# Attention with routed feed-forward on one core: the main loop's matmuls in couples of 64 rows

## The chip, the cores and the metric

The kernel runs on one core of a Trainium2 chip. The metric is the device time of one execution in microseconds (us). Three runs of the kernel before gave 2052.83, 2055.91 and 2057.64 us; the median is 2055.91 us. One more execution was recorded by the hardware profiler; all rows shown here come from that one. TensorE is called PE in the rows, its loading of the stationary operand PEld, VectorE DVE, ScalarE ACT, GpSimd POOL, and the queue that issues transfers SP.

## What is computed

Eight batches of 3136 tokens; `u` and `v` have 256 features a token, `z` has 64. All is float32.

```python
scores = scale * np.matmul(z, z.transpose(0, 2, 1))      # scale = 1 / 3136
attn = np.maximum(scores, 0.0) ** 2
out = np.matmul(attn, v)
x = u * out
...
top_idx = np.argpartition(-(x[b] @ w_gate), 128)[:128]   # for each batch b
xe = x[b, top_idx]
ye = np.maximum(xe @ w1, 0.0) @ w2                       # w1: 256 x 1024, w2: 1024 x 256
x[b, top_idx] += sigmoid(scores of top_idx)[:, None] * ye
```

## The kernel before

**Numbers in two halves.** Every float32 operand of a matmul is split into a high part (rounded to the matmul's type `F32R`) and a low part (the rest). The tensors are `ZH`, `ZL` for `z`, `V[...][w]` with w = 0 (high) and 1 (low) for `v`, and `hi`, `lo` for the squared scores. A product of two such numbers keeps the terms high x high, high x low and low x high.

**Chunks and slots.** The queries of a batch are cut into six chunks of 512 (`CH`) and a last one of 64 (`WHOLE`). The keys are cut into 24 tiles of 128 and one of 64. A slot is a pair of key tiles for one chunk of queries: first its scores, then its products. Since the scores are symmetric, pairs left of the diagonal aren't computed again: the squared scores are turned by DVE, kept in DRAM (`squares`) and fetched (`qk`).

**Scores.** `z` has only 64 features, and a matmul can contract over 128 rows. `ZH` and `ZL` therefore hold their 64 rows twice, in partitions 0 to 63 and 64 to 127, and the moving tile `Z` holds the queries' high part in its upper 64 rows and the low part below, brought there by two transfers a chunk (`bring_z`). One matmul with `ZH` gives high x high plus high x low; a second with `ZL` gives low x high plus low x low. A pair of key tiles takes four matmuls of 512 columns into the two banks of a score tile `sc`; two such tiles exist (`sc_ring`).

**Squares.** ACT reads the score tile (`rise`, `a<-sc`: relu), squares it into `hi`, and then DVE, which multiplies the score tile by `a`, or ACT makes the full square in `a`; only then the score tile is free. POOL or DVE subtracts to make `lo`.

**Products.** The output is kept transposed: 128 features (`h` = 0 or 1) by 512 queries in one PSUM bank `acc`. For each key tile and h there are three matmuls of 128 rows and 512 columns: `V` high and low with `hi`, `V` high with `lo`. Three banks rotate. At a chunk's end DVE multiplies the bank by `ut`, the transposed `u` (`finish`, `evict`).

**The order of the work** is fixed when the program is built: a class `Clock` estimates when each engine would be done, jobs wait in lists for ACT, DVE, POOL and SP, and `choices` takes the next matmul group that would be ready: scores first, then steps of the routing and feed-forward (the `chains`), then products of the current and the next slot. On the chip every engine simply runs its list in order and waits on semaphores. All instructions show one line, L230, that of the recording helper.

Of the kernel before, what the change touches and what calls it, by code (L numbers as in the profile page):

```python
# [18 lines left out]
P = 128  # L19
CH = 512  # L20
GT = 4
# [14 lines left out]
WARM = 6.6  # L36
REST_AT = (2, 5, 7, 9, 12)
# [47 lines left out]
class Clock:  # L85
# [3 lines left out]
    def __init__(self):  # L89
        self.at = {"pe": 0.9, "act": 1.15, "dve": 0.85, "pool": 0.5, "sp": 0.75}  # L90
        self.queue = self.mark = 0.0
        self.writes, self.reads, self.before, self.rings = {}, {}, {}, {}
        self.port = {"dve": (0.0, 0.0), "pool": (0.0, 0.0)}
        self.newest = {}

# [83 lines left out]
    def note(self, by, op, outs, ins):  # L179
# [8 lines left out]
        elif by == "pe":  # L188
# [6 lines left out]
            self.at["pe"] = begin + took + (0.1 if n < 200 else 0.002)  # L195
# [94 lines left out]

class Job:
# [15 lines left out]
def attention_then_routed_ffn(ctx: ExitStack, tc: tile.TileContext, zt, ut, v, wg, w1, w2, cst, cst16, keys, outs, at, cap):  # L307
# [29 lines left out]
    ps_s = Pool(clock, "ps_s", ctx.enter_context(tc.tile_pool(name="ps_s", bufs=2, space=bass.MemoryType.PSUM)), 2)  # L337
# [3 lines left out]
    sc_ring = Ring(ps_s, [P, 2, CH], "sc", 2)  # L341
# [7 lines left out]
    moving_ring = Ring(const, [P, CH], "Z", 2)  # L349
# [4 lines left out]
    banks = [[ps_a, f"acc{i}", None] for i in range(3)]  # L354

    def bank_when():

        free = [clock.idle(x[2][1:]) if x[2] else 0.0 for x in banks if x[2] is None or x[2][0] == "-"]
        return min(free) if free else None

    def take_bank(name):

        x = min((x for x in banks if x[2] is None or x[2][0] == "-"), key=lambda x: clock.idle(x[2][1:]) if x[2] else 0.0)
        got = x[0].tile([P, CH], F32, name=name, tag=x[1])
        x[2] = "+" + got.name
        return got

    def drop_bank(tile_):
        for x in banks:
            if x[2] == "+" + tile_.name:  # L370
                x[2] = "-" + tile_.name
                return
        raise AssertionError(tile_.name)
# [232 lines left out]
    Z = {}  # L606
# [27 lines left out]
    def prep_z(b, i, rank, of=None):  # L634
# [13 lines left out]
        pieces = [slice(0, GT // 2), slice(GT // 2, GT)] if b == i == 0 else [None]  # L648

        def high(e):  # L650
            round_on(e, to[0], src)
            for x in pieces:
                job("pool" if x else "pool|dve", rank, lambda e, x=x: low(e, x), [src, to[0]], took=takes(n))

        def low(e, x):
            at_ = (lambda y: y[:, :, x]) if x else lambda y: y
            rest_on(e, at_(to[1]), at_(src), at_(to[0]))
            if x is pieces[-1]:
                zdone[b, i] = True
                ring.drop(st)  # L660
            for t in range(*x.indices(GT)) if x else ():
                zdone["tile", t] = True
# [16 lines left out]
        free = lambda: b == 0 or (issued > last_key[b - 1, i] and (b - 1, i) in Z)  # L679
        job("act", rank, high, lambda: clock.after(src) + (SLACK if b else 0.05), ok=free)  # L680

    def bring_z(b, c):

        c0, w = CHUNKS[c]
        t = moving_ring.take("Z", F32R)
        Z[b, c] = t[:, :w]
        for rows, z in ((slice(0, 64), ZH), (slice(64, P), ZL)):
            nc.sync.dma_start(t[rows, :w].bitcast(F32), z[rows, c0 : c0 + w].bitcast(F32))

    def first_z():  # L690

        t = moving_ring.take("Z", F32R)
        Z[0, 0] = t
        st = staged["z", 0, 0].rearrange("p (f t a) -> p f t a", t=GT, a=Q)
        to = by_rows(t, 0, CH)
        nc.vector.tensor_copy(to[:64], st[:64])
        nc.vector.tensor_tensor(to[64:], st[64:], by_rows(ZH, 0, CH)[64:].bitcast(F32), op=ALU.subtract)
# [52 lines left out]
    for b in range(B):  # L750
        for c in range(WHOLE):
# [13 lines left out]
            if c < WHOLE - 1:  # L765
                seq.append(half)
# [132 lines left out]

    def own_rest(k, ps):  # L900
# [3 lines left out]
        def rise(e):  # L904
            a_.append(a_ring.take("a"))
            nc.scalar.activation(a_[0][:REST, 0, :REST], ps[:REST, 0, :REST], AF.Relu, scale=SCALE * SCALE)
            job("act", k, high, [a_[0][:REST, 0, :REST]], (), lambda: "own_rest" in consts)

        def high(e):
# [4 lines left out]
            job("dve", k, square, [a, ps[:REST, 0, :REST], st[:REST, :REST]])  # L914

        def square(e):
            a = a_[0][:REST, 0, :REST]
            st = parts[k][0]
            nc.vector.tensor_tensor(a, ps[:REST, 0, :REST], a, op=ALU.mult)
            sc_ring.drop(ps)  # L920
# [6 lines left out]
    def can_score(k):  # L927
        b, c, js, _ = slots[k]
        if k == 0 and not all(("tile", j) in zdone for j in js):
            return False  # L930
        return sc_ring.free() and (b, c) in Z and (k == 0 or all((b, j // GT) in zdone for j in js))

    def score_when(k):
        b, c, js, _ = slots[k]
        t = max([sc_ring.when(), clock.after(Z[b, c])])
        return max([t] + [clock.after(z[:, j * P : (j + 1) * P]) for j in js for z in (ZH, ZL)]) + 0.05

    def half_scores(k):
# [4 lines left out]
        nc.tensor.matmul(ps[:, 0], ZH[:, NJ * P : (NJ + 1) * P], Z[b, c], start=True, stop=True)  # L943
        if k == last_moving[b, c]:
            moving_ring.drop(Z[b, c])
        st = {}

        def shift(e):
# [3 lines left out]
            job("dve", k, total, [st["a"], ps[:REST, 0]])  # L952

        def total(e):
            nc.vector.tensor_tensor(st["s"], ps[:REST, 0], st["a"], op=ALU.add)
            sc_ring.drop(ps)
# [48 lines left out]
        job("act", k, shift, [ps[:, 0]], [a_ring])  # L1005

    def scores(k):
# [4 lines left out]
        mov, w = Z[b, c], CHUNKS[c][1]  # L1012
        if is_second(k):
            mov, w = mov[:, w // 2 :], w // 2
# [8 lines left out]
        if k == last_moving[b, c]:  # L1023
# [1702 lines left out]
```

## Time and profile before

| | |
|---|---|
| median of three runs | 2055.91 us |
| the profiled execution | 2054.14 us |
| its span, first to last instruction | 2052.4 us |
| PE busy (records overlap, so it is no measure of load) | 2041.8 us |
| PEld busy | 1676.7 us |
| DVE, ACT, POOL busy | 1459.0, 1406.9, 1065.8 us |
| mean granted TensorE clock | 1.000 |

A matmul's record reaches from its start to the modelled end of its results; the next one starts before that end. What a matmul costs in a stream is the distance from its start to the next start, called the pitch here.

### The profile page before, as it was taken

The page shows a single profiled execution, that of the slowest core. Times are in us where ns is not written, and L with a number is a line of the kernel's source. Part 1 is how long each engine was busy: PE and PEld are TensorE (multiplying, and loading weights), DVE is VectorE, ACT ScalarE, POOL GpSimd, SP SyncE. Part 2 cuts the span into 40 slices and gives each one's busy share as a digit, 9 for nine tenths or more (in the row PEclk, how much of TensorE's full clock was granted, in tenths as well). Part 3 has the DMA queues.
Part 4 walks back from the last instruction along what each step waited for, and adds up shares of the span by engine and source line. Part 5 has one row for each costly group of instructions (what it writes and reads, how often), then busy time and mean ns, then how long its engine had stood idle before and what let it go on. Part 6 is the DMA issues. An engine that isn't in the chain of part 4 may idle for free. (4 is left out here: it accounts for less than half of the span.)

```text
span 2052.4 us, 29009 instructions
## 1 busy us (share of the span) xinstructions
PE 2041.8 (99%) x9248; PEld 1676.7 (82%) x9248; DVE 1459.0 (71%) x2424; ACT 1406.9 (69%) x1654; POOL 1065.8 (52%) x704
## 2 busy tenths in 40 slices
PE   9999999999999999999999999999999999999998
PEld 7888888888888888888888888888888888888777
DVE  8875577656887568666688666886667666698876
ACT  7875687656876568766777656776678765876652
POOL 6564743447644474245754457433573245754553
PEclk9999999999999999999999999999999999999999
DMA  7898767777678877777777797688777769766774
GB/s 222 245 272 224 191 201 213 209 183 194 195 216 229 209 185 206 221 206 186 197 212 202 207 228 187 210 231 237 190 196 221 203 173 212 214 198 177 185 169 126
DMA packets 430345, 420.00 MB, mean 205 GB/s; under 512 B 131694, under 2 KB 332016, under 8 KB 430192
## 3 DMA queue, kind: packets, MB, share of 16 engines
q1 hardware_dynamic: 429024, 415.66, 75.9%
q0 software_dynamic: 800, 2.10, 0.3%
q8 instruction: 72, 1.18, 0.3%
q14 instruction: 81, 0.66, 0.1%
q10 hardware_dynamic: 368, 0.39, 0.1%
HBM read 230.08 MB, written 175.37 MB: 198 GB/s over the span
## 5 line engine op out<-in xcount | busy, mean ns | idle before, releaser
L230 PE MATMUL acc<-hi,V 128*128 128x512 f32 x4800 | 1214.8, 392 | 0.7 <-ACT hi L230 0.5
L230 PEld LDWEIGHTS acc<-hi,V 128*128 128x128 f32 x4800 | 894.8, 188 | 187.2 <-issue 1.7
L230 POOL TENSOR_TENSOR lo<-qk,hi 128x512 fp32r<-128x512 f32 x287 | 445.3, 1561 | 382.6 <-ACT hi L230 310.0
L230 PE MATMUL acc<-lo,V 128*128 128x512 f32 x2304 | 632.3, 391 | 1.8 <-POOL lo L230 1.8
L230 DVE TENSOR_TENSOR lo<-a,hi 128x1024 fp32r<-128x1024 f32 (+1 forms) x258 | 355.0, 1376 | 252.4 <-ACT a L230 236.2
L230 PEld LDWEIGHTS acc<-lo,V 128*128 128x128 f32 x2304 | 431.5, 188 | 92.3 <-POOL lo L230 2.7
L230 ACT ACTIVATE hi<-a 128x1024 fp32r<-128x1024 f32 (+2 forms) x384 | 366.3, 955 | 175.4 <-PE acc L230 148.5
L230 ACT ACTIVATE a<-sc 128x1024 f32<-128x1024 f32 (+2 forms) x344 | 324.2, 943 | 124.4 <-PE sc L230 107.1
L230 DVE STREAM_TRANSPOSE aT<-a 128x512 f32<-128x512 f32 (+2 forms) x622 | 379.7, 644 | 14.8 <-DMA squares<-aT 13.7
L230 ACT ACTIVATE a<-a 128x1024 f32<-128x1024 f32 (+1 forms) x343 | 327.9, 956 | 63.6 <-DVE a L230 55.4
L230 ACT CAST hi<-qk 128x1024 fp32r<-128x1024 f32 x240 | 251.1, 1048 | 164.3 <-PE acc L230 90.3
L230 PE MATMUL sc<-Z,ZH 128*128 128x512 f32 (+1 forms) x728 | 270.9, 375 | 0.6 <-DVE Z L230 0.6
L230 DVE TENSOR_TENSOR lo<-qk,hi 128x512 fp32r<-128x512 f32 x193 | 184.3, 958 | 119.1 <-ACT hi L230 112.7
L230 POOL TENSOR_TENSOR lo<-a,hi 128x1024 fp32r<-128x1024 f32 (+1 forms) x78 | 175.6, 2252 | 175.9 <-ACT a L230 134.6
L230 PE MATMUL sc<-Z,ZL 128*128 128x512 f32 (+1 forms) x680 | 253.4, 376 | 0.0
L230 POOL TENSOR_TENSOR V<-vst,V 128x512 fp32r<-128x512 f32 (+1 forms) x83 | 125.1, 1521 | 73.2 <-ACT V L230 58.7
L230 PEld LDWEIGHTS sc<-Z,ZH 128*128 128x128 f32 x728 | 136.6, 188 | 27.7 <-DVE Z L230 1.1
L230 PEld LDWEIGHTS sc<-Z,ZL 128*128 128x128 f32 x680 | 129.1, 190 | 26.9 <-POOL ZL L230 0.5
L230 POOL TENSOR_TENSOR lo<-own,hi 128x256 fp32r<-128x256 f32 x94 | 76.8, 838 | 115.0 <-ACT hi L230 95.5
L230 POOL TENSOR_TENSOR ut<-x,w_run 128x1024 f32<-128x1024 f32 x45 | 114.7, 2550 | 30.9 <-DVE x L230 21.2
L230 POOL TENSOR_TENSOR ZL<-zst,ZH 128x512 fp32r<-128x512 f32 (+2 forms) x41 | 51.4, 1254 | 132.6 <-ACT ZH L230 126.6
L230 DVE TENSOR_TENSOR a<-sc,a 128x512 f32<-128x512 f32 (+3 forms) x132 | 99.6, 755 | 18.2 <-ACT hi L230 17.9
(219 smaller groups left out, 1065.5 us busy)
## 6 DMA issues: line engine op xcount, KB each, us to landing
squares<-aT SPq DMA_DIRECT2D x240, 512.0 KB, 4.8
qk<-squares SPq DMA_DIRECT2D x480, 256.0 KB, 6.2
ut<-in_ut SPq DMA_DIRECT2D x48, 512.0 KB, 5.5
vst<-in_v SPq DMA_DIRECT2D x190, 128.0 KB, 4.2
out<-x SPq DMA_DIRECT2D x188, 128.0 KB, 3.6
squares_own<-aT SPq DMA_DIRECT2D x47, 256.0 KB, 2.0
own<-squares_own SPq DMA_DIRECT2D x188, 64.0 KB, 3.0
zst<-in_zt SPq DMA_DIRECT2D x85, 128.0 KB, 6.7
```

The costliest lines, as they stand in the source:

```text
L230: got = real(*args, **kw)
```

## The change

The scores of a pair of key tiles become three couples. In a couple the first matmul uses rows 0 to 63 for the pair's first key tile, the second uses rows 64 to 127 for the other one; each writes a bank of its own. The three terms are high x high, low x high and high x low; low x low is no longer computed. The queries are read where they stand in `ZH` and `ZL`, so the tile `Z`, its transfers and its first filling by DVE are gone.

Every product matmul of the main loop is also cut into two of 64 rows, one for keys 0 to 63 of a tile, one for keys 64 to 127, into two banks (`acc[key][:, 0]` and `[:, 1]`). PSUM holds eight banks: two pairs for `acc`, one pair for scores (before: two), two single ones. At a chunk's end ACT copies the second bank, DVE adds the first one to it, and POOL or DVE multiplies the sum by `ut`. The score pair is free as soon as ACT has read it, since the full square is now made from `a` alone. The matmuls of the last 64 queries (`rest_hl`), the routing and the feed-forward stay at 128 rows; those of a `rest_hl` slot are issued as one block.

```diff
-    sc_ring = Ring(ps_s, [P, 2, CH], "sc", 2)
+    sc_ring = Ring(ps_s, [P, 2, CH], "sc", 1)
+    acc_rings = [Ring(ps_a, [P, 2, CH], f"acc{i}", 1) for i in range(2)]
+    acc_ring = Either(*acc_rings)
+    lend_ring = Either(sc_ring, acc_rings[1])
...
+    HALF = P // 2
+    ROWS = [slice(0, HALF), slice(HALF, P)]
+    one_ring = Ring(ps_m, [P, CH], "one", 1)
...
+    def square_on_dve(a):
+        nc.vector.scalar_tensor_tensor(a, a, 1 / SCALE / SCALE, a, op0=ALU.mult, op1=ALU.mult)
...
-        order = [(q, z) for q in range(n) for z in (ZH, ZL)]
-        if k == 0:
-            order.sort(key=lambda x: x[1] is ZL)
-        for q, z in order:
-            j = js[q]
-            nc.tensor.matmul(ps[:, q], z[:, j * P : (j + 1) * P], mov, start=z is ZH, stop=z is ZL)
...
+        keys_of = P if c < WHOLE else REST
+        terms = (ZH, ZH), (ZL, ZH), (ZH, ZL)
+        for i, (x, y) in enumerate(terms):
+            for q, j in enumerate(js):
+                at_ = slice(j * P, j * P + keys_of)
+                nc.tensor.matmul(ps[:keys_of, q], x[ROWS[q], at_], y[ROWS[q], c0 : c0 + w], start=i == 0, stop=i == len(terms) - 1)
...
             nc.scalar.activation(st["a"], ps, AF.Relu, scale=SCALE * SCALE)
+            sc_ring.drop(ps_)
...
-                nc.vector.tensor_tensor(a, ps, a, op=ALU.mult)
-            sc_ring.drop(ps_)
+                square_on_dve(a)
...
+    def halves_of(x):
+
+        return ROWS[:1] if x[4] == "hl" and x[2] == 1 else ROWS
...
+            acc[key] = acc_ring.take("acc")
+            left[key] = [sum(r in halves_of(y) for y in mine) for r in ROWS]
+        for i, r in enumerate(halves_of(x)):
+            left[key][i] -= 1
+            nc.tensor.matmul(acc[key][:, i], *[y[r] for y in ops], start=start, stop=left[key][i] == 0)
+        if left[key] == [0, 0]:
+            finish(b, c, h)
...
+        def lift(e):
+            st["t"] = sum_ring.take("sum")
+            nc.scalar.copy(st["t"], parts_of[1])
+            job("dve", k, total, [st["t"], parts_of[0]])
+
+        def total(e):
+            nc.vector.tensor_tensor(st["t"], parts_of[0], st["t"], op=ALU.add)
+            acc_ring.drop(acc[b, c, h])
...
+        def weigh(e):
+            xT = chunk[b, c]
+            to = xT[:, h].rearrange("p (f t a) -> p f t a", t=GT, a=Q)
+            ON[e].tensor_tensor(to, st["t"].rearrange("p (t f a) -> p f t a", t=GT, a=Q), to, op=ALU.mult)
...
+            if slots[k][1] == WHOLE:
+                if x is not todo[k][0] or any(operands(k, y) is None for y in todo[k]):
+                    continue
+                t = max(product_when(k, y, operands(k, y)) for y in todo[k])
+                got.append((t, 2 + n * 0.01, ("block", k)))
```

**A chunk's end on PE.** Batch 1, from the last two slots of one chunk to the first of the next. A name such as `acc_3293<-hi_3343,V_2284` says: bank acc_3293, moving operand hi_3343, stationary operand V_2284. Before:

```order
L230 MATMUL acc_3293<-hi_3583,V_2737 128x512 x2
L230 MATMUL acc_3304<-hi_3583,V_2737 128x512 x2
L230 MATMUL sc_3626<-Z_3433,ZH_90 128x512
L230 MATMUL sc_3626<-Z_3433,ZL_91 128x512
L230 MATMUL sc_3626<-Z_3433,ZH_90 128x512
L230 MATMUL sc_3626<-Z_3433,ZL_91 128x512
L230 MATMUL acc_3635<-hi_3588,V_2281 128x512 x4
L230 MATMUL acc_3635<-lo_3597,V_2281 128x512 x2
L230 MATMUL acc_3650<-hi_3588,V_2281 128x512 x4
```

With the change, at the end of such a chunk (here the two last slots are taken bank pair by bank pair):

```order
L243 MATMUL acc_4620<-hi_5007,V_3895 128x512 x8
L243 MATMUL acc_4620<-lo_5033,V_3895 128x512 x4
L243 MATMUL acc_4648<-hi_4982,V_3310 128x512 x8
L243 MATMUL acc_4648<-lo_4991,V_3310 128x512 x4
L243 MATMUL acc_4648<-hi_5007,V_3895 128x512 x8
L243 MATMUL acc_4648<-lo_5033,V_3895 128x512 x4
L243 MATMUL sc_5114<-ZH_90 128x512 x2
L243 MATMUL sc_5114<-ZH_90,ZL_91 128x512 x2
L243 MATMUL sc_5114<-ZL_91,ZH_90 128x512 x2
L243 MATMUL acc_5127<-hi_5039,V_3208 128x512 x8
L243 MATMUL acc_5127<-lo_5048,V_3208 128x512 x4
L243 MATMUL acc_5127<-hi_5098,V_3432 128x512 x4
L243 MATMUL acc_5151<-hi_5039,V_3208 128x512 x8
```

Four score matmuls have become three couples, each product two matmuls. Between the last use of acc_4620 and the first of acc_5127 stand 30 matmuls (15 couples), between acc_4648 and acc_5151 22 (11 couples).

**The last 64 queries of batch 0 on PE**, one slot of `rest_hl` between products. Before:

```order
L230 MATMUL acc_2091<-lo_2221,V_282 128x512
L230 MATMUL acc_2205<-V_282,rest_hl_2242 128x512 x2
L230 MATMUL acc_2205<-V_317,rest_hl_2242 128x512 x2
L230 MATMUL acc_2205<-V_365,rest_hl_2242 128x512 x2
L230 MATMUL acc_2205<-V_389,rest_hl_2242 128x512 x2
L230 MATMUL acc_2078<-hi_2246,V_317 128x512 x4
```

With the change:

```order
L243 MATMUL acc_2941<-lo_3088,V_328 128x512 x2
L243 MATMUL acc_3077<-V_328,rest_hl_3129 128x512 x2
L243 MATMUL acc_3077<-V_390,rest_hl_3129 128x512 x2
L243 MATMUL acc_3077<-V_412,rest_hl_3129 128x512 x2
L243 MATMUL acc_3077<-V_472,rest_hl_3129 128x512 x2
L243 MATMUL acc_2904<-hi_3133,V_390 128x512 x8
```

The block itself is the same eight matmuls of 128 rows; its neighbours now have 64 rows, so PE goes from 64 rows to 128 and back here.

## Rows read from the trace of the kernel before

**Rows 1.** The page: span, busy time and instructions by engine, granted clock in 40 slices.
```profile
span 2052.4 us, 29009 instructions
...
PE 2041.8 (99%) x9248; PEld 1676.7 (82%) x9248; DVE 1459.0 (71%) x2424; ACT 1406.9 (69%) x1654; POOL 1065.8 (52%) x704
...
PEclk9999999999999999999999999999999999999999
```

**Rows 2.** PE's waits: who it waited for, total us, times, longest.
```profile
PE acc L230 <- POOL lo L230: 1.8, 2, 0.9
PE spread L230 <- DVE own L230: 1.4, 1, 1.4
```

**Rows 3.** PE's groups by shape: count, busy us, mean ns, idle before.
```profile
L230 PE MATMUL acc<-hi,V 128*128 128x512 f32 x4800 | 1214.8, 392 | 0.7 <-ACT hi L230 0.5 <-DVE hi L230 0.2
L230 PE MATMUL acc<-lo,V 128*128 128x512 f32 x2304 | 632.3, 391 | 1.8 <-POOL lo L230 1.8
L230 PE MATMUL sc<-Z,ZH 128*128 128x512 f32 x626 | 244.9, 392 | 0.6 <-DVE Z L230 0.6
L230 PE MATMUL sc<-Z,ZL 128*128 128x512 f32 x578 | 226.8, 393 | 0.0
...
L230 PE MATMUL sc<-Z,ZL 128*128 128x256 f32 x94 | 24.4, 282 | 0.0
...
L230 PE MATMUL sc<-Z,ZL 128*128 128x64 f32 x8 | 2.2, 276 | 0.0
```

**Rows 4.** PE in order of time near 1438 us: start, length, matmuls.
```profile
1437.96 0.39 PE L230 MATMUL sc<-Z,ZH 128*128 128x512 f32 x1
...
1438.87 0.63 PE L230 MATMUL y<-wh,hh 128*128 128x256 f32 x4
1439.34 0.64 PE L230 MATMUL y<-wl,hh 128*128 128x256 f32 x4
```

**Rows 5.** PE in order of time near 7 us, bf16 matmuls that fill a wait.
```profile
7.47 2.33 PE L230 MATMUL idle<-zero 128*128 128x512 bf16 x10
```

**Rows 6.** A weight load's mean ns by group, and PE near 2021 us.
```profile
L230 PEld LDWEIGHTS acc<-hi,V 128*128 128x128 f32 x4800 | 894.8, 188 | 187.2 <-issue 1.7 <-ACT hi L230 1.0 <-DVE hi L230 0.5
...
L230 PEld LDWEIGHTS turned<-c_sb,ut 128*128 128x128 f32 x8 | 0.9, 140 | 0.5 <-issue 0.5
...
2020.69 1.04 PE L230 MATMUL turned<-c_sb,ut 128*128 128x128 f32 x8
2021.56 0.39 PE L230 MATMUL old<-diag,c_sb 128*128 128x128 f32 x2
```

**Rows 7.** PE in order of time: short matmuls, one of 64 rows among them.
```profile
2017.13 0.26 PE L230 MATMUL ids<-what,oh 128*128 128x5 bf16 x4
2017.25 0.17 PE L230 MATMUL ids<-io,oh 128*128 128x5 bf16 x1
2017.27 0.47 PE L230 MATMUL acc<-lo,V 128*128 128x512 f32 x1
2017.58 0.39 PE L230 MATMUL acc<-V,own_rest 128*128 128x512 f32 x1
...
2035.69 0.25 PE L230 MATMUL ids<-c,oh 128*128 128x2 bf16 x4
...
2035.87 0.17 PE L230 MATMUL ids<-c,oh 64*128 64x2 bf16 x1
...
2035.98 0.18 PE L230 MATMUL ids<-io,oh 128*128 128x2 bf16 x1
```

**Rows 8.** DVE, ACT and POOL groups: count, busy us, mean ns, idle before.
```profile
L230 DVE TENSOR_TENSOR ut<-acc,ut 128x512 f32<-128x512 f32 x96 | 64.1, 673 | 15.6 <-PE acc L230 15.5
...
L230 DVE TENSOR_TENSOR lo<-a,hi 128x1024 fp32r<-128x1024 f32 x224 | 319.5, 1427 | 248.6 <-ACT a L230 236.2 <-issue 6.5 <-POOL xr L230 2.6
...
L230 ACT ACTIVATE hi<-a 128x1024 fp32r<-128x1024 f32 x289 | 306.5, 1061 | 138.7 <-PE acc L230 121.5 <-ACT a L230 7.3 <-issue 4.5
L230 ACT ACTIVATE a<-sc 128x1024 f32<-128x1024 f32 x289 | 294.9, 1021 | 107.7 <-PE sc L230 90.4 <-DVE aT L230 13.2 <-PE tot L230 2.2
...
L230 ACT COPY row<-spread 128x512 f32<-128x512 f32 x3 | 1.8, 608 | 1.5 <-PE spread L230 1.5
...
L230 POOL TENSOR_TENSOR lo<-qk,hi 128x512 fp32r<-128x512 f32 x287 | 445.3, 1561 | 382.6 <-ACT hi L230 310.0 <-DMA qk<-squares 18.5 <-DMA own<-squares_own 13.5
```

More of the change, by code (lines that the diff above doesn't have):

```diff
@@ L94, in __init__ @@
         self.newest = {}
+        self.half, self.by_half, self.long = [0.0, 0.0], False, False
     @staticmethod
@@ L194, in note @@
                 took *= 2
-            self.at["pe"] = begin + took + (0.1 if n < 200 else 0.002)
+            first, stop = self.span(ins[0])[:2]
+            one = stop - first == P // 2
+            mine = [first // (P // 2)] if one else [0, 1]
+            begin = max([begin] + [self.half[g] for g in mine])
+            if one != self.by_half:
+                begin = max([begin] + self.half) + (0.1 if self.long else 0.0)
+                took = took + 0.108 if n >= 200 else max(took, 0.119)
+            after = 0.002 if n >= 200 or one != self.by_half else 0.1
+            self.by_half, self.long = one, n >= 200
+            for g in mine:
+                self.half[g] = begin + took + after
+            self.at["pe"] = max(begin, min(self.half))
             end = begin + took + 0.175
@@ L288, in drop, with __init__, free, when @@
         raise AssertionError(tile_.name)
+class Either:
+    def __init__(self, *rings):
+        self.rings = rings
+    def free(self):
+        return any(x.free() for x in self.rings)
+    def when(self):
+        return min(x.when() for x in self.rings if x.free())
+    def take(self, name, dt=F32):
+        return min((x for x in self.rings if x.free()), key=lambda x: x.when()).take(name, dt)
+    def drop(self, tile_):
+        for x in self.rings:
+            if any(y[0] == tile_.name and y[1] for y in x.held):
+                return x.drop(tile_)
+        raise AssertionError(tile_.name)
 class Job:
@@ L353, in attention_then_routed_ffn, with spares @@
     half_ring = Ring(vpool, [P, 2, NK, P], "Vr", 1)
-    banks = [[ps_a, f"acc{i}", None] for i in range(3)]
+    HALF = P // 2
+    ROWS = [slice(0, HALF), slice(HALF, P)]
+    one_ring = Ring(ps_m, [P, CH], "one", 1)
+    spare = []
+    def spares():
+        if not spare and now[0] < kmax and slots[now[0]][:2] == (B - 1, WHOLE) and acc_rings[0].free():
+            t = acc_rings[0].take("spare")
+            spare.extend([t[:, i], False] for i in range(2))
+        return [x for x in spare if not x[1]]
     def bank_when():
-        free = [clock.idle(x[2][1:]) if x[2] else 0.0 for x in banks if x[2] is None or x[2][0] == "-"]
+        free = [one_ring.when()] if one_ring.free() else []
+        free += [clock.free(x[0]) for x in spares()]
         return min(free) if free else None
     def take_bank(name):
[L363 to L366, printed above, removed]
+        free = [(one_ring.when(), 0, None)] if one_ring.free() else []
+        free += [(clock.free(x[0]), 1 + i, x) for i, x in enumerate(spares())]
+        x = min(free, key=lambda x: x[:2])[2]
+        if x is None:
+            return one_ring.take(name)
+        x[1] = True
+        return x[0]
     def drop_bank(tile_):
-        for x in banks:
-            if x[2] == "+" + tile_.name:
-                x[2] = "-" + tile_.name
+        for x in spare:
+            if x[0] is tile_:
+                x[1] = False
                 return
-        raise AssertionError(tile_.name)
+        one_ring.drop(tile_)
     pending = {e: [] for e in ("act", "dve", "pool", "sp")}
@@ L677, in low, with z_free @@
                 ring.drop(st)
[L679 to L697, printed above, removed]
+        job("act", rank, high, lambda: clock.after(src) + (SLACK if b else 0.05), ok=lambda: b == 0 or z_free(b, i))
+    def z_free(b, i):
+        return issued > max(last_key[b - 1, i], last_moving[b - 1, i])
     def stage_v(b, g, queues=None):
@@ L2620, in emit @@
             wake(x)
+        elif what[0] == "block":
+            k = what[1]
+            for x in todo[k]:
+                multiply(k, x, operands(k, x))
+            todo[k] = []
+            advance_slots()
         else:
@@ L2627, in emit, with advance_slots @@
                     hi_ring.drop(parts[k][0])
-            while now[0] < kmax and not todo.setdefault(now[0], products(now[0])):
-                finished_slot(now[0])
-                now[0] += 1
-                begin_slot()
+            advance_slots()
+    def advance_slots():
+        while now[0] < kmax and not todo.setdefault(now[0], products(now[0])):
+            finished_slot(now[0])
+            now[0] += 1
+            begin_slot()
     def finished_slot(k):
```

148 lines of the change are left out of this document (74 added, 74 removed).

## The prediction

> **What bounds the kernel now.** I read the page first: PE is busy in 99% of a span of 2052.4 us, at full granted clock in all 40 slices, while DVE, ACT and POOL stand at 71, 69 and 52% [rows 1]. Busy time on PE is no load, so I looked at its waits: the largest sum for any one cause is 1.8 us [rows 2]. PE is never kept waiting; what counts is how many matmuls it has and at what pitch they go. The groups by shape give the number: 7104 products and 1204 score matmuls of 512 columns, each 391 to 393 ns from start to end [rows 3]. The pitch comes from the timeline: four score matmuls of 512 columns from 1437.96 to 1438.87 us, 0.2275 each; four of 256 columns from 1438.87 to 1439.34, 0.1175 each [rows 4]. The 8308 at 0.2275 alone are 1890 us. So the time is a count times a pitch, and a change is priced by what it does to either.
>
> **What it removes.** Of the 626 + 578 score matmuls of 512 columns [rows 3], 48 belong to the half key tile (626 less 578); the others are 289 pairs of key tiles with four matmuls each. Four become three couples. If a couple takes the slot of one matmul, 289 x 0.2275 = 65.7 us go. The 47 pairs of 256 columns (94 + 94 matmuls, [rows 3] shows half of them) save 47 x 0.1175 = 5.5 us. Sum 71.2. The eight score matmuls of 64 columns that are added (three singles for two matmuls a batch) cost about 1 us, at the 0.1 to 0.2 that such short ones take.
>
> **The pitch of a couple** is the unknown that decides. After the change 8019 slots of 512 columns remain: 4800 products with `hi` (96 of them one half alone), 2304 with `lo`, 867 couples for pairs and 48 for half tiles. One nanosecond a slot is 8 us. No row of before shows two matmuls of 64 rows side by side, so I bound it. Three things have to fit. First, the columns: 512 stream through either half; if the halves are independent, that is the 0.2275 of now. A pitch below that is possible: bf16 matmuls of 512 columns go at 0.216 (ten in 2.33 us, of which the last one's own 0.39, the length of any matmul of 512 columns, is taken off, over nine [rows 3, 5]), so 0.0115 of today's pitch is not columns and might be hidden behind the other half. Second, weight loads: a couple needs two. One lasts 188 ns, but loads follow each other closer than that: eight transposes go at (2021.56 - 2020.69)/8 = 0.109 us, each with a load of its own of 140 ns [rows 6]. Two are 0.218, under 0.2275, with little to spare. With the 188 ns kind the closest that I have is 0.1175 [rows 4], there set by 256 columns; two of those would be 0.235. Third, that the halves do run together at all. I take 0.2275: the nearest row that is bound by loads allows it, and the columns give it. The range keeps 0.216 and 0.235.
>
> **Changes of height.** The order of the changed program goes from 64-row to 128-row matmuls and back 125 times, 250 changes: 45 visits are the short counting matmuls of the routing, 29 are blocks of the last 64 queries, the others gates, transposes, feed-forward. One place of before shows the price: five short bf16 matmuls stand 0.03 apart (2017.13 to 2017.25 for four), but the one of 64 rows starts some 0.10 after the one ahead of it (2035.69 + 0.25 - 0.17 for the last of four, then 2035.87) and the next of 128 rows 0.11 later [rows 7]. That is 0.07 to 0.08 more each way: 250 x 0.08 = 20 us. Besides, a long matmul behind a short or idle stretch finds its weights not yet loaded: 2017.27 to 2017.58 is 0.31 in place of 0.2275 [rows 7], 0.08 more. Behind short visits this is paid now already; about 100 more such places make 8 us. Total 28. Bounds: nothing, if PE hides it; or a full wait for the matmul's end and then a bare load, 0.392 - 0.2275 + 0.188 = 0.35 each, 88 us [rows 3, 6].
>
> The Trainium skill, TensorEngine Tiling (Array Packing), section Tiling Modes, says that changing the tiling mode drains TensorE. By it alone, with a drain as what a matmul's record has beyond its pitch (392 - 227.5 = 165 ns), the 250 changes would be an estimated 41 us in place of 20; the gap around the 64-row matmul is shorter than that, so I stay with the row.
>
> **The ends of chunks.** Before, a bank is free after one DVE multiplication of 0.673. Now ACT copies (0.608, as `row<-spread`), then DVE adds (0.673): 1.28, and with one operation ahead on either engine (1.061 on ACT, 1.427 on DVE) at worst 3.8 [rows 8]. The cover is the 15 and 11 couples shown with the change: 3.4 and 2.5 us. So most of it is hidden, some is not: 96 bank pairs at 0 to 1.3 us, bounds 0 and 125. **Scores** now have one pair of banks, free after ACT's read of 1.021, at most one operation later [rows 8], 2.1; in the order at the chunk's end shown, 24 couples (5.5 us) of products stand between two sets of scores. I take 10 us for both together, since most chunk ends have cover for half an operation ahead on each engine (1.28 + 0.53 + 0.71 = 2.5).
>
> **Work at no cost.** 96 ACT copies are 58 us, less 13 squares that leave ACT; the 96 multiplications with `ut` go to POOL (67, about 105 us at the 1.561 of a POOL operation of that size) or DVE. 47 + 48 added DVE operations on half tiles and squares change DVE by some 40 us. That gives shares near 74, 72 and 60% of 2022 us for DVE, ACT and POOL; the cover is PE's 2000 us of matmuls, and were it gone, the time would be DVE's 1500. The 110 transfers of `Z` leave SP; the one wait for `Z`, 0.6 us, was for its first filling by DVE [rows 3], so they were hidden.
>
> **Sum.** 2054.1 (the profiled execution, 1.8 us or 0.1% under the median of the three) - 71.2 + 1 + 28 + 10 = 2021.9. I say 2023, with the median in mind.
>
> **Rivals.**
> 1. *Weight loads become the bound, slower.* Place: every couple. If two loads of the 188 ns kind need 2 x 0.1175, the pitch is 0.235 and 8019 x 0.0075 = 60 us come back: 2083. It decides from a pitch of 0.2275 + 32/8019 = 0.2315 on. For it: PEld is at 82% with one load a matmul. Against: loads at 0.109. Chance 0.11.
> 2. *The halves don't run together, or loads go one after another at their full length.* A couple is then 0.455 or 0.376: 2023 + 8019 x 0.2275 = 3847, or 2023 + 8019 x 0.1485 = 3214. Against the second: loads of 188 ns at a pitch of 0.1175 overlap today [rows 4, 6]. Nothing in the trace speaks for or against the first. Chance 0.05.
> The Trainium skill, TensorE: Matmul & The Clock Gate, section LDWEIGHTS, has a load's time go by its columns and not its rows; by that rule halving the rows makes no load shorter, which is what rivals 1 and 2 need. No run here shows it yet.
> 3. *Couples go closer than a matmul now*, at 0.216: 8019 x 0.0115 = 92 less, 1931. For it: the bf16 pitch; against: nothing says that the 0.0115 is idle time of a half. Chance of under 1985: 0.09.
> 4. *Bank pairs and changes of height cost what was saved.* At 0.7 us a chunk end more (67) or 0.35 a change (60 more) the time is 2082 to 2090. For it: the cover is only as long as the mean eviction. Chance of ending slower this way 0.05; of ending within 0.2% of before, 0.05.
>
> **How the numbers follow.** The forecast (1985 to 2050) has 0.65, the four rivals what stands there. A range of 1985 to 2085 leaves out rival 2, most of rival 3 and what of rivals 1 and 4 is above it, together not over 0.2. A measurement of this kernel can tell about 0.2%, 4 us, from no change: faster 0.74 (forecast and rival 3), same 0.05, slower 0.21.
>
> **What would show it.** Right: PE's matmuls of a couple start in a steady rhythm of two in 0.2275 us, PE's waits for ACT and DVE stay under some 15 us in total, and gaps of 0.1 to 0.2 stand where 128-row matmuls begin and end. Wrong: a rhythm away from 0.2275 in long runs of products, where nothing waits; or sums of tens of us of PE waiting for the add into `sum` or for `a<-sc`.

## The result, and the profile after

The changed kernel takes 2076.63 us (median of 2073.97, 2076.63 and 2078.20; one more run, of 6464.95 us, took three times as long and is left out), the kernel before, in the same place, 2054.37. The ratio of the means is 1.0105, 95% interval 1.0082 to 1.0128: **slower by about 1%**, where 1.5% faster was forecast. The time lies in the range, its sign is wrong. The profiled execution took 2073.97 us, 19.8 more than that of before.

The page of the kernel after, to be set beside [rows 1]: span, then busy time by engine.
```profile
span 2072.2 us, 44494 instructions
...
PE 2033.8 (98%) x16981; PEld 1665.4 (80%) x16981; DVE 1610.8 (78%) x2477; ACT 1443.0 (70%) x1750; POOL 1223.3 (59%) x793
```
PE and PEld, now with 1.8 times the instructions, are busy for slightly less time: two halves work at once. DVE has 152 us more to do and POOL 158, in a span that is 20 longer. The mean granted clock is 0.999 in this execution and 0.998 and 0.996 in the two other runs; in the runs of the kernel before that stand beside the experiments below it is 1.000.

PE's groups by shape, beside [rows 3], and its loads, beside [rows 6]:
```profile
L243 PE MATMUL acc<-hi,V 64*128 64x512 f32 x9504 | 1294.6, 391 | 9.2 <-DVE sum L243 8.1 <-POOL V L243 0.8
L243 PE MATMUL acc<-lo,V 64*128 64x512 f32 x4608 | 707.6, 389 | 3.8 <-DVE lo L243 2.5 <-POOL lo L243 1.2
L243 PE MATMUL sc<-ZH 64*128 64x512 f32 x626 | 147.1, 402 | 8.8 <-ACT a L243 6.6 <-DVE G L243 1.6 <-DVE a L243 0.2
...
L243 PEld LDWEIGHTS acc<-hi,V 64*128 64x128 f32 x9504 | 954.0, 184 | 189.4 <-DVE sum L243 22.3 <-issue 9.6 <-POOL V L243 2.4
```
PE in order of time near 800 us:
```profile
800.66 1.07 PE L243 MATMUL acc<-lo,V 64*128 64x512 f32 x8
801.57 0.40 PE L243 MATMUL sc<-ZH 64*128 64x512 f32 x2
801.80 0.39 PE L243 MATMUL sc<-ZH,ZL 64*128 64x512 f32 x2
802.03 0.40 PE L243 MATMUL sc<-ZL,ZH 64*128 64x512 f32 x2
802.26 0.62 PE L243 MATMUL acc<-hi,V 64*128 64x512 f32 x4
```
Three couples take 802.26 - 801.57 = 0.69 us, 0.23 each, and four couples of `lo` 0.91, 0.2275 each: the pitch of one matmul of before. So the columns were saved as forecast. PE's waits, beside [rows 2], show where the time went instead:
```profile
PE acc L243 <- DVE sum L243: 8.1, 12, 1.5
PE sc L243 <- ACT a L243: 6.6, 5, 3.0
PE acc L243 <- POOL rest_hl L243: 4.7, 4, 1.7
PE acc L243 <- DVE lo L243: 2.5, 4, 0.6
PE sc L243 <- DVE G L243: 1.6, 1, 1.6
```
Before, no cause of a wait had over 1.8 us; all the rows of PE's waits together come to some 6 us before and some 34 after, where the prediction would have had under 15. A wait also costs more than its row says. The row counts idle time from the modelled end of the last matmul, which lies 0.392 - 0.2275 = 0.165 us behind the time at which the next one would have started; and the second couple behind a stop starts late, its weights not loaded. One stop of each kind, from PE's timeline:
```profile
244.66 0.39 PE L243 MATMUL acc<-hi,V 64*128 64x512 f32 x2
246.22 2.14 PE L243 MATMUL acc<-V,rest_hl 128*128 128x512 f32 x8 [1.18 <-POOL rest_hl L243]
248.29 1.67 PE L243 MATMUL acc<-hi,V 64*128 64x512 f32 x12
249.80 1.09 PE L243 MATMUL acc<-lo,V 64*128 64x512 f32 x8
```
246.22 - 244.66 - 0.2275 = 1.33 us are lost where the row has 1.18. Then eight matmuls of 128 rows take 2.07 where eight pitches are 1.82, so 0.25 more, and the six couples behind them 1.51 where six pitches are 1.365, 0.145 more. DVE's groups, beside [rows 8]:
```profile
L243 DVE TENSOR_TENSOR lo<-a,hi 128x1024 fp32r<-128x1024 f32 x222 | 336.9, 1518 | 159.4 <-ACT a L243 151.2 <-issue 4.5 <-PE acc L243 1.7
...
L243 DVE TENSOR_TENSOR sum<-acc,sum 128x512 f32<-128x512 f32 x96 | 65.4, 683 | 18.4 <-ACT sum L243 18.1
...
L243 DVE SCALAR_TENSOR_TENSOR a<-a 128x1024 f32<-128x1024 f32 x42 | 59.2, 1414 | 6.1 <-ACT hi L243 6.0
...
L243 DVE SCALAR_TENSOR_TENSOR a<-a 128x512 f32<-128x512 f32 x47 | 46.2, 982 | 12.3 <-ACT hi L243 12.3
```
`lo<-a` takes 1518 ns where it took 1427, with POOL busier beside it.

### The profile page after: what moved, and what is told of

It is laid out like the page before. It is cut to its first block, busy times and chain, and to the rows that moved or that the text cites. A ratio compares the mean times of both kernels' runs of the same rounds, so it can differ in the third digit from the quotient of the medians.

```text
span 2072.2 us, 44494 instructions
## 1 busy us (share of the span) xinstructions
PE 2033.8 (98%) x16981; PEld 1665.4 (80%) x16981; DVE 1610.8 (78%) x2477; ACT 1443.0 (70%) x1750; POOL 1223.3 (59%) x793
## 4 chain that ended last, share of the span: by engine, by line
PE 68%; DVE 8%; DMA 6%; issue 3%; ACT 3%; POOL 2%; SPq 1%; POOLq 0%; DVEq 0%; ACTq 0%
PE acc L243 58%; PE sc L243 8%; DVE lo L243 2%; DMA qk<-squares 2%; DVE aT L243 2%; ACT a L243 1%; DMA squares<-aT 1%; ACT hi L243 1%; DVE a L243 1%; DMA vst<-in_v 1%; DMA ut<-in_ut 1%; SPq L243 1%; POOL lo L243 1%; PE h L243 1%; DVE sum L243 1%
## 5 line engine op out<-in xcount | busy, mean ns | idle before, releaser
L243 PE MATMUL acc<-hi,V 64*128 64x512 f32 x9504 | 1294.6, 391 | 9.2 <-DVE sum L243 8.1
L243 PEld LDWEIGHTS acc<-hi,V 64*128 64x128 f32 x9504 | 954.0, 184 | 189.4 <-DVE sum L243 22.3
L243 PE MATMUL acc<-lo,V 64*128 64x512 f32 x4608 | 707.6, 389 | 3.8 <-DVE lo L243 2.5
L243 PEld LDWEIGHTS acc<-lo,V 64*128 64x128 f32 x4608 | 484.8, 184 | 84.9 <-DVE lo L243 6.6
L243 PE MATMUL sc<-ZH 64*128 64x512 f32 (+1 forms) x728 | 163.8, 387 | 9.4 <-ACT a L243 6.6
L243 POOL TENSOR_TENSOR ut<-sum,ut 128x512 f32<-128x512 f32 x67 | 98.7, 1474 | 113.6 <-DVE sum L243 95.6
L243 PE MATMUL sc<-ZL,ZH 64*128 64x512 f32 (+1 forms) x728 | 159.6, 376 | 0.0
L243 PE MATMUL sc<-ZH,ZL 64*128 64x512 f32 (+1 forms) x680 | 139.2, 371 | 0.0
L243 DVE SCALAR_TENSOR_TENSOR a<-a 128x512 f32<-128x512 f32 (+2 forms) x97 | 107.6, 1111 | 18.5 <-ACT hi L243 18.4
L243 PEld LDWEIGHTS sc<-ZH 64*128 64x128 f32 x728 | 79.7, 184 | 37.0 <-ACT a L243 14.5
```

The lines of the kernel that those rows point to most:

```text
L243: got = real(*args, **kw)
```

## The experiments

The theory at the outset: each visit from the 64-row loop to 128-row work and back costs more than was counted, and chunk ends cost the rest. The rivals: the slower DVE work, or slips in the fixed order that a better one would remove. All medians are of 4 or 10 runs beside runs of the kernel before of 2053.2 to 2056.2 us.

**1. More visits.** One of the products with `lo` in each slot stays a matmul of 128 rows: 576 such matmuls, no change in columns.
```diff
     def halves_of(x):
+        if x[4] == "lo" and x[0] == 1 and x[3] == 1:
+            return [slice(0, P)]
```


> In every slot of two key tiles one of the products with lo is issued as one matmul of 128 rows into the first bank, in place of a couple; the result is the same and so are the columns. That adds 576 visits to 128 rows, 1152 changes of height. If a visit costs about 0.3 us (two gaps of 0.1 and one load that isn't hidden), as the trace after suggests: 2077 + 173 = 2250. If the visits are what ate the whole gain (92 us over 125 visits, 0.74 each): 2500. If changes of height cost next to nothing and waits for other engines ate the gain: under 2110.

2286.04 us, ratio 1.1135 (1.1117 to 1.1154), 209.4 more. In the order of the trace 48 of the 576 matmuls stand beside other work of 128 rows, so the visits rise by 528 and not by 576 (656 in place of 128): **0.40 us a visit**. PE's groups show the weights that aren't there in time, in the length of the visiting matmul and of the first score couples:
```profile
L243 PE MATMUL acc<-lo,V 128*128 128x512 f32 x576 | 288.0, 500 | 0.0
L243 PE MATMUL sc<-ZH 64*128 64x512 f32 x626 | 165.6, 484 | 3.7 <-ACT a L243 3.6
```
500 ns where the same matmul had 391 [rows 3].

**2. More columns.** A fourth couple, low x low, in each set of scores.
```diff
-        terms = (ZH, ZH), (ZL, ZH), (ZH, ZL)
+        terms = (ZH, ZH), (ZL, ZH), (ZH, ZL), (ZL, ZL)
```


> The scores get a fourth couple, low x low, as many columns as before the change: 289 couples of 512 and 47 of 256 columns more, 71 us. If PE's own work sets the pace through the whole loop: 2077 + 71 = 2148. If PE waits for the other engines some 50 us in the loop, part of the added work falls into those waits: 2095 to 2125.

2145.68, 1.0450 (1.0433 to 1.0468): 69.1 more for 71 us of columns. PE's own work sets the pace; added work doesn't disappear in the waits, so what three couples save is really saved.

**3. Chunk ends as before.** At a chunk's end DVE multiplies the first bank at once; no copy, no addition, no work on POOL. The second bank's half of the products is missing from the output.
```diff
-        job("act", k, lift, [acc[b, c, h]], [sum_ring])
+        job("dve", k, weigh, ready, ok=lambda: (b, c) in chunk)
```


> At a chunk's end DVE multiplies the first bank by ut at once, as before the change; the second bank is left out of the sum (so half of the products are missing from the output). No ACT copy, no add, no POOL multiplication: 96 of each go. If the ends of chunks are where PE waits, the waits for the add (8 us) and the loads and slips behind them go: 2045 to 2060. If they aren't: 2070 to 2077.

2053.75, 1.0000 (0.9991 to 1.0010): 22.9 less. The two banks cost **23 us**, 0.24 for each of 96. That is the price of everything that hangs on them: the run also takes 96 copies off ACT, 67 multiplications off POOL and 29 off DVE, and other waits fall with them, PE's for `a` from ACT from 6.6 us to 1.5.

**4. The slower square taken off DVE.**
```diff
-            on = "dve" if second else "dve|act"
-            job(on, k, square, [a, hi], took={...})
+            job("act", k, square, [a, hi])
```


> All full squares are made by ACT, none by DVE (89 and 8 small ones move): DVE loses about 105 us of work whose operands lie all in SBUF, ACT gains about 80. If PE waits because DVE and POOL have become slower at making lo since that square reads SBUF alone: 2050 to 2065, and DVE's lo of 512 columns goes back from 1.18 towards 0.96 us. If that isn't the cause: 2077 or, with ACT at 74%, a few us more.

2084.83, 1.0154 (1.0137 to 1.0171): 8.2 more, although DVE's busy time falls from 1610.8 to 1518.6. ACT has the squares now, and PE waits 6.6 us for `V` from ACT, which is not among the waits of the changed kernel. So moving the square doesn't pay; whether its slowness costs anything is told by run 15. `lo<-a` stays at 1513 ns.

**5. Scores alone.** The kernel before with three couples a pair of key tiles, products left in 128 rows. Each set of scores is then a visit of its own, 335 in all.
```diff
-            nc.tensor.matmul(ps[:, q], z[:, j * P : (j + 1) * P], mov, start=z is ZH, stop=z is ZL)
+            for i, (x, y) in enumerate(terms):
+                for q, j in enumerate(js):
+                    at_ = slice(j * P, (j + 1) * P)
+                    nc.tensor.matmul(ps[:, q], x[half[q], at_], y[half[q], c0 : c0 + w], start=i == 0, stop=i == len(terms) - 1)
```


> One part alone: the kernel before, with two score pairs and three banks of one h as it has them, but the scores of a pair of key tiles in three couples of 64 rows, read in place; products stay at 128 rows, so there is no ACT copy and no add at a chunk's end. It saves the same 71 us of columns and makes 335 visits (to 64 rows here). At the 0.36 us a visit that the run with extra visits showed: 2054 - 71 + 121 = 2104. If that run's price came from something else than the change of height, and visits are nearly free: 1985 to 2010.

2119.88, 1.0313 (1.0296 to 1.0330): 63.7 more than before. With 71 saved, 335 visits cost 135, **0.40 each**. PE's timeline shows one cycle of it:
```profile
800.10 0.50 PE L230 MATMUL sc<-ZH 64*128 64x512 f32 x2
800.44 0.40 PE L230 MATMUL sc<-ZH,ZL 64*128 64x512 f32 x2
800.67 0.39 PE L230 MATMUL sc<-ZL,ZH 64*128 64x512 f32 x2
800.99 2.11 PE L230 MATMUL acc<-hi,V 128*128 128x512 f32 x8
802.95 1.08 PE L230 MATMUL acc<-lo,V 128*128 128x512 f32 x4
803.95 0.50 PE L230 MATMUL sc<-ZH 64*128 64x512 f32 x2
```
3 + 12 pitches of 0.2275 are 3.41 us; the cycle takes 3.85. The missing 0.44 stands in four places: 0.34 to the second couple (0.11 too much), 0.32 to the first 128-row matmul (0.09), 1.96 for eight (0.14), 1.00 for four (0.09).

**6 and 7. Both kernels without routing and feed-forward**, whose matmuls make 95 of the 125 visits.
```diff
-    cap = int(moe_capacity)
+    cap = 0 * int(moe_capacity)
```


> The kernel before without routing and feed-forward (capacity taken as 0): the output is u times attention alone. It is the yardstick for the next run; from the trace, the routing's and feed-forward's matmuls and the end behind the last product are some 70 to 90 us: 1965 to 1985.

> The changed kernel without routing and feed-forward, in the same way: 30 visits are left of 125. If visits and chunk ends explain the loss, 95 visits less the exposed loads that they cost before already, some 30 us, leave it: the kernel is then 71 - 30 x 0.36 - 24 = 36 us faster than the run before it. If the loss sits in the loop itself (one score pair, slower DVE and POOL), it is there as well: 0 to 15 us slower than the run before it.

1985.28 before (0.9658 of the whole kernel, 0.9641 to 0.9674) and 1986.55 after (0.9661, 0.9645 to 0.9677). The difference falls from 22 to 1.3 us: the visits of routing and feed-forward and what the change does to the rest of their work are 21. But 71 us of columns less, 30 visits more (12) and the chunk ends (23) should make the changed one 36 us faster there. It isn't, so some 37 are lost elsewhere in the loop. PE's waits show most of it. Before:
```profile
PE acc L230 <- POOL lo L230: 1.9, 3, 0.9
```
After:
```profile
PE acc L243 <- DVE sum L243: 8.8, 15, 1.2
PE sc L243 <- ACT a L243: 8.6, 11, 2.9
PE acc L243 <- POOL rest_hl L243: 8.3, 7, 2.0
PE acc L243 <- DVE lo L243: 4.5, 7, 0.6
```
Those for `sum` belong to the chunk ends. The other 25 come to 21.4 us, and to 28 with the 0.27 behind each that was read above (0.165 for the end that the row doesn't count, 0.11 for the second couple's load). The granted clock has a part too: 0.996 in all four runs of 7, 0.999 in those of 6, an estimated 6 us of 1986 if PE had work throughout.

**8. More cover at a chunk's end.** The first two slots of a chunk, too, are taken bank pair by bank pair.
```diff
-            if (first and (b or c)) or k >= ends[b, c] - 1:
+            if (b or c) and k <= begins[b, c] + 1 or k >= ends[b, c] - 1:
```


> The first two slots of a chunk are taken bank pair by bank pair too, in place of the first alone, so that more products stand between the last use of a bank pair and its next use (in the order, a median of 3.3 us in place of 2.8 at a pitch of 0.2275; the middle of the short ones 2.6 in place of 2.4). If waits for the add at chunk ends cost 24 us: 2060 to 2070. If what the run with one bank saved was ACT's and DVE's work instead: 2077.

2072.34, 1.0082 (1.0065 to 1.0099): 4 us less than the changed kernel. The intervals of the two overlap, but the same edit gives 3 us in run 10 and 5 in run 14.

**9 to 11. A more careful order.** `choices` takes a matmul group only 0.8 us after its operands should be there (9); this with the cover of 8 (10); this with the single bank of 3, its half of the products again missing (11).
```diff
-        t = max(clock.after(y) for y in ops) + 0.05
+        t = max(clock.after(y) for y in ops) + 0.8
```


> The same operations; only the order of PE's matmuls differs: a score set, a product or a block of the last 64 queries is taken into the order 0.8 us after its operands or its bank should be ready, in place of 0.05. Visits stay (252 changes of height). If some 40 us of the loss are short waits of PE for ACT, DVE and POOL that come a little later than the order assumes: 2040 to 2060, and PE's waits fall from 34 us in all to under 15. If the waits only move to other places: 2070 to 2085.

> Both the margin of the run before it and the first two slots of a chunk bank pair by bank pair. If both act on the same waits at chunk ends: within 4 us of the run with the margin alone. If they act on different ones: 3 to 6 us less than that.

> The margin, and the second bank left out at a chunk's end (half of the products are missing from the output). If chunk ends and late operands are separate losses, they add up: the run with the margin less 10 to 20 us, and what then stays of the 71 us that the columns save is the price of the visits, some 35 to 40 us: 2020 to 2035. If the margin alone removes the waits at chunk ends: the same as the run with the margin.

2089.25 (1.0176, 1.0158 to 1.0193), 2086.43 (1.0156, 1.0139 to 1.0173) and 2065.40 (1.0052, 1.0035 to 1.0069). Waiting in the plan makes other waits: PE's for `V` from ACT, not among those of the changed kernel, now have 11.8 us in run 9, and all its waits 48.7 in place of 34. The clock fell more as well: 0.994 in its profile in place of 0.999, an estimated 10 us of 2087, so the 12.6 us that run 9 loses aren't the price of its waits alone. That a margin of 0.8 us takes the waits away is refuted; a smaller one was not tried. The chunk ends come out at about the same again (2089.25 - 2065.40 = 23.9).

**12 to 14. The block of the last 64 queries.** POOL made its `rest_hl` 23 times out of 24, and the stop at 246.22 above waits for one that POOL began 0.57 us after ACT's part was there, behind a `lo`, and that took 1.71 us. It goes to DVE alone (12); the products are no longer taken as a block (13); 12 with the cover of 8 (14).
```diff
-            job("pool|dve", k + 0.1, lambda e: low(e, by[:, 1], src, by[:, 0]), [src, by[:, 0]], took=takes(CH))
+            job("dve", k + 0.1, lambda e: low(e, by[:, 1], src, by[:, 0]), [src, by[:, 0]], took=takes(CH))
...
-            if slots[k][1] == WHOLE:
-                if x is not todo[k][0] or any(operands(k, y) is None for y in todo[k]):
-                    continue
...
-            elif ops is not None:
+            if ops is not None:
```


> The changed kernel with the low part of rest_hl made on DVE only, not on POOL or DVE as the order chooses. In the changed kernel POOL took it 23 times of 24 at about 1.7 us each where DVE needs 0.69, and four waits of 4.7 us together stand in front of the block of rest_hl products. Theory A (these waits, with about 0.27 us behind each, are part of the open 33 us): 5 to 10 us less, 2067 to 2073. Theory B (the scheduler's order only moves the wait to DVE's other work, since DVE is 78% busy): within 4 us of the changed kernel, 2073 to 2081.

> The changed kernel with the rest_hl products of a long slot issued one by one as each is ready and no longer as one block that waits until all of its operands are there. The number of changes of height stays at 250. If waiting for the whole block costs (theory A): 3 to 8 us less, 2069 to 2074. If the waits only come at the later product (theory B): no difference beyond 3 us, 2074 to 2081.

> The changed kernel with both edits: rest_hl's low part on DVE only, and the first two slots of a chunk issued bank pair by bank pair, which by itself gave 5 us. If the two stalls are separate the gains add up: 2060 to 2068. If one only covers the other: 2068 to 2073. Neither theory has it beat the kernel before (2054), since visits at 0.36 to 0.40 us and chunk ends at 24 us stay in.

2076.82 (1.0100, 1.0083 to 1.0117), 2077.25 (1.0106, 1.0089 to 1.0123) and 2071.39 (1.0082, 1.0065 to 1.0099): nothing gained but the cover's 4 to 5 us. The waits of run 12 say why:
```profile
PE sc L243 <- ACT a L243: 8.0, 6, 3.0
PE acc L243 <- DVE sum L243: 7.8, 12, 1.2
PE acc L243 <- DVE lo L243: 5.4, 3, 2.4
PE acc L243 <- DVE rest_hl L243: 4.5, 6, 1.1
```
The wait for `rest_hl` has only changed its releaser from POOL to DVE, and `lo` from DVE comes later than before (5.4 us in place of 2.5).

**15 and 16. One score pair, in the kernel before.** First the early release of a pair and the square from SBUF, with two pairs as before (15); then with one pair (16).
```diff
             nc.scalar.activation(st["a"], ps, AF.Relu, scale=SCALE * SCALE)
+            sc_ring.drop(ps_)
...
-                nc.vector.tensor_tensor(a, ps, a, op=ALU.mult)
-            sc_ring.drop(ps_)
+                nc.vector.scalar_tensor_tensor(a, a, 1 / SCALE / SCALE, a, op0=ALU.mult, op1=ALU.mult)
...
-    sc_ring = Ring(ps_s, [P, 2, CH], "sc", 2)
+    sc_ring = Ring(ps_s, [P, 2, CH], "sc", 1)
```


> The kernel before with one part of the change alone: a score pair is given back right after ACT's relu has read it, and DVE makes its squares from the tile in SBUF alone. Two score pairs as before, products in 128 rows. If the slower square on DVE matters (theory B): 3 to 10 us more than before. If not (theory A): within 3 us of 2054.

> The same kernel with one score pair in place of two, its banks left empty. Theory A (the single score pair makes PE wait at each batch's same places, and is 10 to 15 us of the open 33): 8 to 18 us more than the run with two pairs. Theory B (the single pair is covered by products, the open part is elsewhere): within 4 us of it.

2055.12 (1.0007, 0.9997 to 1.0017) and 2079.99 (1.0128, 1.0100 to 1.0155). The square from SBUF costs nothing that can be told; **the second score pair is worth 25 us**, more than either theory said; some 5 of these are clock (0.998 and 0.997 in the runs of 16, 1.000 in all but one of those of 15). In the two profiled executions (spans 2057.7 and 2077.4) some 10 of the 20 us lie ahead of the last product of the loop and some 10 behind it. Waits of run 16:
```profile
PE sc L230 <- DVE a L230: 5.1, 5, 2.5
PE ids L230 <- DVE oh L230: 4.5, 1, 4.5
PE sc L230 <- ACT a L230: 3.9, 4, 1.6
```
The first and the third are in the loop, 9.0 us in nine waits; with 0.27 behind each 11.4. In the changed kernel the waits of `sc` for `a` and `G` have about the same size (9.0 in eight). In three of them, 4.4 us together, ACT had itself been waiting for DVE, which still had to turn an older tile `a`; before the longest one ACT stood still for 6.45 us:
```profile
80.98 1.02 ACT L243 ACTIVATE a<-sc 128x1024 f32<-128x1024 f32 x1 [6.45 <-DVE aT L243]
```
So what a single score pair needs cover for is DVE's list as well as ACT's. The 4.5 of run 16 are at the end of the program, where PE has nothing else to run until a step of the routing is there. The changed kernel, whose lending may take a bank pair of `acc` too, has no such wait there, but its end is also longer: from the last `lo` product to the end of the span 41.1 us (last of these at 2031.1) in place of 35.1 (2017.27, [rows 7], to 2052.4).

## Why the prediction was wrong

- **The columns and the pitch: right.** 71.2 us were to go at a couple's pitch of 0.2275. The timeline has that pitch, and run 2 has 69.1 for as many columns put back. Rivals 1, 2 and 3 fall: loads of 184 ns, two for each couple, don't bound it, since PEld is busy for 80% of the span with almost twice the loads, so those of the two halves overlap; and couples follow each other at 0.227 us in the median and 0.2288 on average, the matmuls before at 0.227 and 0.2281. The Trainium skill, TensorE: Matmul & The Clock Gate, section LDWEIGHTS, says that a load goes by its columns and not its rows; the trace agrees (184 ns with 64 rows, 188 with 128 [rows 6]).
- **Changes of height: the mechanism right, the size a little short.** 28 us were counted for 125 visits. The distances from start to start of all matmuls in the trace, less their pitch (each half by itself, counted half), give about 26 us at the changes and 13.5 at the 125 second couples behind them: 39, of which some 8 were paid before as loads behind short matmuls. That leaves 31; by the price of runs 1 and 5, 0.40 for visits of a long matmul, it would be 42. What was short is the load of the second matmul (0.11), counted for some 100 places at 0.08; it stands behind every visit, and behind the first matmul of a long one too. The Trainium skill, TensorEngine Tiling (Array Packing), section Tiling Modes, has a change of mode drain TensorE. The estimate by it was 41 us for the 250 changes in place of 20; the trace has 26 at the changes alone, so it lies nearer to the row than to the estimate.
- **Chunk ends and scores, the step that failed.** "I take 10 us for both together": run 3 has 23 for the chunk ends alone, and run 16, with the changed kernel's own waits, some 10 for the single score pair in the loop. The bound of "one operation ahead on either engine" was not one. ACT, DVE and PE at a chunk's end of the changed kernel, in order of time:
```profile
1269.38 6.46 DVE L243 TENSOR_TENSOR V<-vst,V 128x512 fp32r<-128x512 f32 x1
...
1273.32 0.59 ACT L243 COPY sum<-acc 128x512 f32<-128x512 f32 x1 [0.67 <-PE acc L243]
...
1275.76 1.21 DVE L243 SCALAR_TENSOR_TENSOR a<-a 128x1024 f32<-128x1024 f32 x1
...
1276.89 0.68 DVE L243 TENSOR_TENSOR V<-vst,V 128x512 fp32r<-128x512 f32 x1
...
1277.50 0.68 DVE L243 TENSOR_TENSOR sum<-acc,sum 128x512 f32<-128x512 f32 x1
...
1278.23 1.19 PE L243 MATMUL acc<-hi,V 64*128 64x512 f32 x8 [1.54 <-DVE sum L243]
```
The copy is done at 1273.91, but DVE is in an operation that lasts 6.46 us, then takes two more, and adds at 1277.50: a bank pair is free 4.9 us after its copy began, not 1.28. Over the 96 evictions this time is 1.97 us in the median and 4.86 at most. Most fit under the cover of 11 to 15 couples; PE waited for 12, and the six longest, over 3.6 us each, lie beyond it. Ahead of all six, and of three of the others, stand DVE operations that took at least 0.6 us longer than the shortest of their form. DVE's subtractions for `V` and its additions into `sum` have the same size (shortest, median and longest in ns, then the first and last start):
```profile
L243 DVE TENSOR_TENSOR V<-vst,V x28: 673/1366/6457, 9.2 to 1812.4; 128x512 fp32r<-128x512 f32 x28
L243 DVE TENSOR_TENSOR sum<-acc,sum x96: 647/682/695, 56.1 to 2032.7; 128x512 f32<-128x512 f32 x96
```
The one at 1269.38 took 6457, and POOL was busy beside it for 5.90 of the 6.46 us. `lo<-a` of 1024 columns takes 1.22 us on average and 1.23 at most in the 78 cases in which POOL does nothing meanwhile, and 1.97 on average, up to 3.75, in the 83 in which POOL is at work for over half of the time; the additions, of which one operand lies in PSUM, never go over 0.695. So the prediction's "one operation ahead" was wrong in the number of operations and in the length of one. Rival 4 had the right place. That its sum came close (2082 to 2090 named, 2077 measured) is in part luck: the chunk ends cost a third of the 67 us it had for them, the changes of height 3 to 14 over the 28 in place of 60, and the rest comes from terms that no rival had. Its chance of 0.10 was too low.
- **"Work at no cost": wrong.** It had DVE some 40 us up; it is 152. The 40 were right for the work itself. The lengths of DVE's operations, added up, rise by 156 us; measured against the shortest operation of the same form in either trace, 40 of these are work and 116 are operations that take longer (214 us above the shortest before, 330 after), beside a POOL with 158 us more to do. DVE is not the bound by its sum, and run 4 shows that relief in one place doesn't help, but `lo`, `rest_hl` and `sum` come late in a fixed order. By the waits (for `lo`, `rest_hl` and `V` 9.2 us in ten) with 0.27 behind each, late operands cost some 12 us where before they had some 3. That DVE's fuller list makes them late is argued from run 12, where the wait moves to the next operand; that POOL's work makes DVE's operations longer is read from the traces. No run takes POOL's added work away and leaves all else: the chunk-end multiplications on DVE alone were not tried.
- **The end of the program**, 6 us longer, had no term in the sum, and neither had **the granted clock**: 0.999, 0.998 and 0.996 in the three runs of the changed kernel, 1.000 before. At 2 us for each 0.001 that is an estimated 2 to 8 us, if PE had work throughout.

Together: -71 for columns, 31 to 42 for visits, 23 for chunk ends, some 10 for the score pair, some 9 for late operands, 6 at the end, and some 5 for a pitch that is on average 0.7 ns longer: +13 to +24, without the clock. The measured difference is 22.3 between medians and 19.8 between the profiled executions. That the sum fits is no proof of its terms. They come from different kernels, and the waits in them overlap: 23, 10 and 9 are 42, but at the places where PE waited the distances from start to start, less the pitch, grow by only some 33 us (from 7 to 40). One order differs from the next by up to 5 us. What is shown is that visits (31 to 42) and waits (some 33) ate the 71; how the waits divide among chunk ends, score pair and late operands is not settled. No version beats the kernel before; with the whole change, runs 8 and 14 come nearest, 16 and 17 us behind. A second score pair in the changed kernel was not tried: the change has given its banks to `acc`.

## What to carry to other kernels

Where PE never waits, a change that takes matmuls away and gives up banks trades a sure gain against cover: price the banks first, by taking one away in the kernel as it is (25 us here for one pair, 10 of them in the loop, and 23 for a longer eviction, against 71 saved). For a buffer's cover take the longest list that can stand ahead of the operation that frees it, not one operation, and each operation at the longest that the trace has for it, not at its mean; and add to each wait what the idle time in the trace doesn't show. Mixing matmuls of 64 and 128 rows costs some 0.40 us a visit, more than one and a half matmuls of 512 columns, so it pays only in long runs of either.

## What was not expected of the hardware

After 4.47 us in which PE did nothing, run 16 shows the granted clock at 0.50, the level of 1.2 GHz, for some 6 us, and matmuls of 256 columns go at 0.214 us in place of 0.1175 [rows 4]. Busy time by stretch, with the clock in the third column from the right:
```profile
2046.50:2051.00 4.50, 0.03 (x2) 0.01 (x1) 3.89 (x24) 0.88 (x2) 0.00 (x0) 0.92 0.06 15
2051.00:2053.40 2.40, 2.40 (x12) 1.18 (x13) 1.29 (x2) 0.00 (x0) 0.99 (x1) 0.50 0.00 0
2053.40:2057.10 3.70, 3.70 (x18) 3.69 (x17) 0.00 (x0) 0.00 (x0) 0.00 (x0) 0.50 0.14 40
2057.10:2077.00 19.90, 17.30 (x122) 14.50 (x120) 4.73 (x9) 3.75 (x7) 2.95 (x3) 1.00 0.05 21
```
So a wait is paid there a second time, by the work behind it: 18 matmuls in those 3.7 us would take 2.1 at full clock. How long PE stood still doesn't tell it alone. In the same run a wait of 2.52 us is followed by 3.2 us at a clock of 0.52:
```profile
548.30:551.50 3.20, 3.15 (x8) 2.48 (x9) 1.71 (x3) 2.28 (x3) 0.15 (x1) 0.52 0.50 169
```
In the changed kernel a wait of 2.96 us at 82.06 us is followed by 4 us at 1.00, and in run 13, whose wait at the same place lasts 2.99, it is followed by this:
```profile
82.60:86.00 3.40, 2.93 (x14) 2.34 (x16) 3.37 (x5) 3.29 (x5) 0.00 (x0) 0.50 0.88 307
```
The mean clock also differs from run to run of one program, from 0.996 to 0.999 in the changed kernel.

The two halves of a couple run as two queues: their starts at first lie 3 to 4 ns apart and drift to some 100 ns, and their loads overlap: one by one they add up to 3129 us, and PEld is busy for 1665. That is why PEld's share fell with almost twice the loads.
